# Negated maxima sent earlier, loads and stores given behind them, weight conversions in two halves: a block-sparse attention and feed-forward kernel

## The chip, the cores and the metric

The kernel runs as one launch on one core of one Trainium2 chip. The metric is the time of the launch on the device in microseconds (us); the median of several runs counts. The engines are named as in the profile: PE (matrix products), PEld (its weight loads), DVE (vector), ACT (scalar), POOL (GpSimd) and SP (which here only issues DMA transfers). On-chip memory is SBUF; products of PE land in PSUM, eight banks of 128 x 512 words.

## What is computed

Attention over 4 batches of 8 heads, 768 positions, 64 numbers per position, with a mask by blocks of 32 positions; its output is the input of a feed-forward part.

```python
scores = scale * np.matmul(q, k.transpose(0, 1, 3, 2))
...
mask = np.abs(blk_i - blk_j) <= window
mask = mask | (blk_i == 0) | (blk_j == 0) | (blk_i == n_blocks - 1) | (blk_j == n_blocks - 1)
...
scores = np.where(mask, scores, -1000000000.0)
scores = scores - np.max(scores, axis=-1, keepdims=True)
attn = np.exp(scores)
attn = attn / (np.sum(attn, axis=-1, keepdims=True) + 1e-09)
return np.matmul(attn, v).astype(np.float32)
...
h = x @ w_in
g = h - np.tanh(h)
return (g @ w_out).astype(np.float32)
```

The feed-forward part takes the 3072 positions as rows of 512 numbers, and its weights are 512 x 2048 and 2048 x 512. The weights arrive as 64-bit words and are turned into 32-bit ones by integer operations on DVE.

## The kernel before

The 32 heads are worked in 16 **pairs**. A head has three **double tiles** n (96 in all): two tiles of 128 rows against 768 columns, which take three PSUM banks of 512 columns. So a pair has six double tiles. For each double tile n:

- `smax` makes the masked scores once, roughly (one product of 88 rows per piece), into a bank, and `most` takes the maximum of each row from it on DVE (tile mc). This runs about six double tiles (one pair) ahead of use: the constant LEAD is 12, and a double tile lasts two units of the order's time.
- `scores` makes them again, finely: two products per piece, of which the second reads 89 rows of a **slot**. Row 88 of the slot holds the negated maximum, so the product delivers scores less their maximum. `exps` takes the exponential on ACT (tile pe), `high` (ACT, ph) and `low` (POOL, pl) split it into two halves of 16 bits, and `accum` multiplies these with v on PE.

Behind the three double tiles of a head in `smax`, the maxima go into row 88: `most_join` (DVE, tile mj), `most_turn` (PE, a transposition into a PSUM bank) and `most_send`: DVE negates and scales (tile nm), and SP sends the 3 KB into the slot. The second product of the next `scores` that needs this head waits for that transfer.

Ahead of that, a pair's inputs are prepared: `load_x` fetches q and k (tile rawx, 768 KB), `mask_words` and `low_words` split them on DVE in three parts each (the upper words into a PSUM bank, the lower into tile lo), `dist` sends them into the pair's slot in twelve transfers of 192 KB (letters A to D from rawx, c and d from lo). `load_v` fetches v (tile rawv, 384 KB); `v_most`, `v_turn`, `v_scale` and `v_parts` scale it by its maximum (tile am) and split it into the tile vhl. `norm` divides the output of a head by its sum (tile xq), and `spill` stores the output of a pair (384 KB) to `xscr` in memory.

Beside the attention, six pieces of weights are loaded (`load_pre`, 512 KB each, in tile rawi or rawo, one every 24 units) and converted by `convert_pre`, in three operations of DVE over 512 columns (`convert_op`), with a PSUM bank in between. The result (tile cvti or cvto) is stored to memory (`wt`) and read when the attention ends.

**What sets the order.** All engine instructions of the attention are written out by a list of due times: `at(time, f, *args)` puts a step into the list, the list is sorted, and the class `InOrder` (its line 79 issues everything, which is why the profile shows L79) keeps each engine to this program order. A pair has 12 units. The times decide the order alone; when a step runs is decided by waits. Six PSUM banks are given out in turn (`bank()`) to `scores`, `smax`, `mask_words`, `most_turn`, `v_turn` and the conversions, so a step that is moved also changes who waits for whose bank. SP issues its transfers in that order, and one behind another.

The first pairs have shifts of their own (LATE), and `smt(n)` spreads the first 24 double tiles. Behind the attention (from about 415 us) the feed-forward part runs, whose code the change doesn't touch.

## Time and profile before

| | us |
|---|---|
| median of 3 runs | 967.9 (965.65 to 968.12) |
| profiled execution | 962.25 |
| its span | 960.2 |
| PE busy | 891.2 |
| DVE busy | 736.6 |
| ACT busy | 642.7 |
| POOL busy | 474.8 |

The profile is of one execution. In the row of DMA below, the span is cut into 40 slices of 24 us, and each digit is the share in tenths that the 16 DMA engines were busy: they are nearly full during the attention (the first 17 slices) and mostly idle afterwards.

```
PE   2798899899989989779999999999999999999997
DVE  6798999899999977279999766766666675666664
ACT  0587889899989989855666665555555565555453
DMA  8946778877877783343622120310010010001001
```

### The profile page before, as it was taken

The numbers are of one execution on the slowest core, as the hardware profiler recorded it, in microseconds if no ns is written. First come the engines' busy times: TensorE is split into PE (matmuls) and PEld (weight loads), VectorE is DVE, ScalarE is ACT, GpSimd is POOL, SyncE is SP. The second block draws the span as 40 slices with busy tenths as digits, with TensorE's granted clock in tenths as the row PEclk, the third lists the DMA queues.
The fourth block names the chain that finished last, engine by engine and source line by source line (L and its number), as shares of the span: only waits on it lengthen the run. The fifth ranks groups of instructions, "written<-read, shape, count | busy, mean of one in ns | idle before, by whom it ended". The sixth has DMA issues, their size and how long they took to land.

```text
span 960.2 us, 18142 instructions
## 1 busy us (share of the span) xinstructions
PE 891.2 (93%) x7072; PEld 740.1 (77%) x7072; DVE 736.6 (77%) x1254; ACT 642.7 (67%) x1045; POOL 474.8 (49%) x231
## 2 busy tenths in 40 slices
PE   2798899899989989779999999999999999999997
PEld 1676778787878778667888788888888888888885
DVE  6798999899999977279999766766666675666664
ACT  0587889899989989855666665555555565555453
POOL 1376889788989888934455322222222222222221
PEclk9998999999999999889999999999999999999999
DMA  8946778877877783343622120310010010001001
GB/s 212 215 106 172 190 200 206 195 198 201 200 192 192 194 177 115 107 141 118 193 94 75 39 63 1 110 34 1 20 58 0 1 44 1 1 0 45 1 1 44
DMA packets 54101, 99.75 MB, mean 104 GB/s; under 512 B 5768, under 2 KB 26440, under 8 KB 54016
## 3 DMA queue, kind: packets, MB, share of 16 engines
q1 hardware_dynamic: 53704, 97.81, 38.3%
q8 instruction: 55, 0.90, 0.4%
q10 hardware_dynamic: 312, 0.79, 0.3%
q14 instruction: 30, 0.25, 0.1%
HBM read 44.64 MB, written 15.20 MB: 62 GB/s over the span
## 4 chain that ended last, share of the span: by engine, by line
PE 73%; DVE 11%; DMA 7%; ACT 4%; issue 3%; POOL 1%; SPq 0%; DVEq 0%; ACTq 0%; POOLq 0%
PE pf L563 25%; PE ps L79 24%; PE pf L595 8%; PE pf L596 8%; PE pf L597 8%; DMA slot<-nm 3%; DVE mc L79 3%; ACT pe L79 2%; DVE ps L79 2%; DMA slot<-lo 1%; PE pf L477 1%; DVE vhl L79 1%; POOL pl L79 1%; DMA slot<-rawx 1%; DVE pf L579 1%
## 5 line engine op out<-in xcount | busy, mean ns | idle before, releaser
L79 POOL TENSOR_TENSOR pl<-pe,ph 128x1536 f16<-128x1536 f32 x96 | 308.0, 3214 | 90.6 <-ACT ph L79 67.2
L79 PE MATMUL ps<-slot 89*128 89x512 f32 (+5 forms) x1152 | 254.0, 365 | 43.4 <-DMA slot<-nm 14.3
L586 POOL TENSOR_TENSOR gl<-t,gh 128x512 fp32r<-128x512 f32 x94 | 121.4, 1292 | 346.0 <-ACT gh L585 290.3
L79 PEld LDWEIGHTS ps<-slot 89*128 89x128 f32 (+2 forms) x1152 | 182.3, 199 | 72.1 <-DMA slot<-nm 18.2
L79 DVE TENSOR_REDUCE mc<-ps 128x1 f32<-128x512 f32 (+1 forms) x288 | 188.4, 682 | 31.1 <-PE ps L79 29.0
L79 ACT ACTIVATE pe<-ps 128x512 f32<-128x512 f32 x288 | 166.1, 588 | 42.0 <-PE ps L79 37.8
L79 ACT ACTIVATE ph<-pe 128x768 f16<-128x768 f32 x192 | 161.8, 843 | 5.6
L578 DVE TENSOR_TENSOR t<-t,pf 128x512 f32<-128x512 f32 x94 | 64.4, 685 | 124.6 <-ACT t L572 124.6
L585 ACT ACTIVATE gh<-t 128x512 fp32r<-128x512 f32 x94 | 59.4, 632 | 118.8 <-DVE t L582 118.7
L79 PEld LDWEIGHTS <-ph 128*128 128x128 f16 x2304 | 112.9, 99 | 25.8 <-issue 25.3
L79 PE MATMUL ps<-vhl,ph 128*128 128x65 f16 (+1 forms) x2304 | 124.7, 197 | 2.5 <-DVE vhl L79 1.9
L79 PE MATMUL ps<-vhl,pl 128*128 128x65 f16 x1152 | 119.6, 195 | 5.5 <-POOL pl L79 5.5
L79 PEld LDWEIGHTS <-pl 128*128 128x128 f16 x1152 | 109.0, 101 | 7.9 <-POOL pl L79 7.9
L570 ACT ACTIVATE u<-pf 128x512 f32<-128x512 f32 x94 | 56.2, 598 | 77.1 <-PE pf L563 76.4
L595 PE MATMUL pf<-wx,gh 128*128 128x512 f32 x192 | 74.7, 389 | 0.0
L596 PE MATMUL pf<-wx,gh 128*128 128x512 f32 x192 | 74.7, 389 | 0.0
L582 DVE COPY_PREDICATED t<-mk,pf 128x512 f32<-128x512 int32 x94 | 69.5, 740 | 6.6
L581 DVE SCALAR_TENSOR_TENSOR pf<-qq,pf 128x512 f32<-128x512 f32 x94 | 65.2, 693 | 7.8 <-DVE pf L580 0.5
L563 PE MATMUL pf<-slot,wx 128*128 128x512 f32 x288 | 70.3, 391 | 0.4 <-DVE t L582 0.4
L563 PE MATMUL pf<-xbuf,wx 128*128 128x512 f32 x288 | 69.5, 390 | 0.0
L574 ACT ACTIVATE qq<-u,bias 128x512 f32<-128x512 f32 x94 | 68.3, 727 | 0.0
L576 ACT ACTIVATE mk<-u,bias 128x512 f32<-128x512 f32 x94 | 67.8, 721 | 0.0
(113 smaller groups left out, 1468.5 us busy)
## 6 DMA issues: line engine op xcount, KB each, us to landing
slot<-rawx SPq DMA_DIRECT2D x128, 192.0 KB
slot<-lo SPq DMA_DIRECT2D x64, 192.0 KB
rawx<-kq SPq DMA_DIRECT2D x15, 768.0 KB
stage<-w_in SPq DMA_DIRECT2D x13, 512.0 KB
stage<-w_out SPq DMA_DIRECT2D x13, 512.0 KB
rawv<-v SPq DMA_DIRECT2D x16, 384.0 KB
xscr<-xq SPq DMA_DIRECT2D x16, 384.0 KB
out<-ob SPq DMA_DIRECT2D x24, 256.0 KB
```

The lines of the kernel that those rows point to most:

```text
L79: r = f(*args, **kw)
L563: nc.tensor.matmul(h, lhsT=w[:, cc], rhs=x[:, c, :], start=(k == 0), stop=(k == 3 * NCT - 1))
L574: nc.scalar.activation(out=qq, in_=u, func=AF.Square, scale=QS, bias=qbias)
L576: nc.scalar.activation(out=mk, in_=u, func=AF.Relu, scale=-1.0, bias=tbias)
L578: nc.vector.tensor_tensor(out=t, in0=t, in1=h, op=ALU.subtract)
L581: nc.vector.scalar_tensor_tensor(out=h, in0=qq, scalar=QC, in1=h, op0=ALU.add, op1=ALU.mult)
L582: nc.vector.copy_predicated(t, mk.bitcast(I32), h)
L585: nc.scalar.activation(out=gh, in_=t, func=AF.Copy)
L586: nc.gpsimd.tensor_tensor(out=gl, in0=t, in1=gh.bitcast(F32), op=ALU.subtract)
L595: nc.tensor.matmul(o, lhsT=gh[:, c], rhs=wo[0][ft], start=(ft == f0), stop=False)
L596: nc.tensor.matmul(o, lhsT=gh[:, c], rhs=wo[1][ft], start=False, stop=False)
L597: nc.tensor.matmul(o, lhsT=gl[:, c], rhs=wo[0][ft], start=False, stop=(ft == f1 - 1))
```

## The change

Four numbers in the list of due times, and a split. The load of x stands 1.8 units later (-34.2 for -36), the store of xq 3.2 units later (19.6 for 16.4). From the fifth head on, the turn of the maxima and their sending stand 1.2 units sooner (`late` 0.8 for 2). And each weight conversion is done in two halves of 256 columns, the second four units behind the first, each with three operations and a bank of its own; the store stands behind the second half.

```diff
-        at(t0 - 36 + late[0] if pr > 1 else -18.5 if pr else -49, load_x, pr)
+        at(t0 - 34.2 + late[0] if pr > 1 else -18.5 if pr else -49, load_x, pr)
...
-        at(t0 + 16.4, spill, pr)
+        at(t0 + 19.6, spill, pr)
...
-        late = 0 if h < 4 else 2
+        late = 0 if h < 4 else 0.8
         at(t0 + 1.6, most_join, h)
         at(t0 + 2.5 + late, most_turn, h)
         at(t0 + 2.75 + late, most_send, h)
...
-    def convert_pre(m, ft, k):
+    def convert_pre(m, ft, e, k):
         if k == 0:
-            wcv[m, ft] = f2.tile([P, 512], I32, tag="wcvt", name=f"cvt{m}{ft}")
-            wcp[0] = bank().bitcast(I32)
-        convert_op(nc, wraw[m, ft], wcv[m, ft], wcp[0], k)
-        if k == 2:
+            if e == 0:
+                wcv[m, ft] = f2.tile([P, 512], I32, tag="wcvt", name=f"cvt{m}{ft}")
+            wcp[0] = bank()[:, 0:256].bitcast(I32)
+        convert_op(nc, wraw[m, ft][:, 512 * e : 512 * (e + 1)], wcv[m, ft][:, 256 * e : 256 * (e + 1)], wcp[0], k)
+        if e and k == 2:
             nc.sync.dma_start(out=wt[m, ft], in_=wcv.pop((m, ft)).bitcast(F32))
...
-        for k in range(3):
-            at(W0 + DW * x + 6.05 + 0.45 * k, convert_pre, "io"[x % 2], x // 2, k)
+        for e in range(2):
+            for k in range(3):
+                at(W0 + DW * x + 6.05 + 4 * e + 0.45 * k, convert_pre, "io"[x % 2], x // 2, e, k)
```

**SP's queue in pair 9**, from nm of an odd head (nm19) on to the load of x behind; `slot2_75<-rawx11` and `slot2_75<-lo11` are the transfers of pair 11's q and k, `rawo1<-w_out` is a weight load, `xscr2<-xq8` the store of pair 8, `rawv11` the load of v. Before:

```order
L79 DMA slot0_73<-nm19_4021 1x6x128
L79 DMA slot2_75<-rawx11_3518 64x768 x2
L79 DMA xscr2_62<-xq8_3873 768x1x128
L79 DMA slot2_75<-rawx11_3518 64x768 x2
L79 DMA rawo1_4167<-w_out 128x1024
L79 DMA slot2_75<-rawx11_3518 64x768 x2
L79 DMA rawv11_4226<-v 128x768
L79 DMA slot1_74<-nm20_4232 1x6x128
L79 DMA slot2_75<-rawx11_3518 64x768 x2
L79 DMA slot2_75<-lo11_3745 64x768 x2
L79 DMA rawx13_4357<-kq 128x1536
```

After:

```order
L79 DMA slot0_73<-nm19_4010 1x6x128
L79 DMA rawx12_4016<-kq 128x1536
L79 DMA slot1_74<-lo10_3327 64x768
L79 DMA slot2_75<-rawx11_3595 64x768 x4
L79 DMA rawo1_4175<-w_out 128x1024
L79 DMA slot2_75<-rawx11_3595 64x768
L79 DMA slot1_74<-nm20_4222 1x6x128
L79 DMA xscr2_62<-xq8_3882 768x1x128
L79 DMA slot2_75<-rawx11_3595 64x768
L79 DMA rawv11_4239<-v 128x768
L79 DMA slot2_75<-rawx11_3595 64x768 x2
```

Both nm stand further ahead: the store, one of the slot transfers and the load of v now stand behind nm20, and the load of x (rawx12) stands behind nm19, where it stood ahead of it.

**SP's queue early**, about nm2 (head 2), which is not moved. Before:

```order
L79 DMA rawx3_420<-kq 128x1536
L79 DMA rawv2_434<-v 128x768
L79 DMA slot2_75<-rawx2_241 64x768
L79 DMA slot1_74<-nm2_489 1x6x128
L79 DMA slot2_75<-rawx2_241 64x768 x5
```

After:

```order
L79 DMA rawv2_432<-v 128x768
L79 DMA slot2_75<-rawx2_277 64x768
L79 DMA slot1_74<-nm2_487 1x6x128
L79 DMA rawx3_495<-kq 128x1536
L79 DMA slot2_75<-rawx2_277 64x768 x5
```

The load of x for pair 3 went from ahead of nm2 to behind it.

**DVE at a conversion**, in pair 6 (rawo0 is the weight piece, mc14 the maxima of head 14, nm13 the negated maxima of head 13, am7 the maximum of v). Before:

```order
L79 TENSOR_SCALAR ps3_97<-rawx8_2260 128x512
L79 TENSOR_TENSOR lo8_2483<-rawx8_2260,ps3_97 128x512
L79 TENSOR_SCALAR ps5_99<-rawo0_2489 128x512
L79 TENSOR_REDUCE mc14_2690<-ps2_96 128x2
L79 SCALAR_TENSOR_TENSOR ps5_99<-rawo0_2489,ps5_99 128x512
L79 TENSOR_REDUCE mc14_2690<-ps0_94 128x1
L79 SCALAR_TENSOR_TENSOR cvto0_2699<-rawo0_2489,ps5_99 128x512
L79 TENSOR_REDUCE mc14_2690<-ps2_96 128x1
L79 TENSOR_REDUCE am7_2762<-rawv7_2548 128x1
L79 TENSOR_SCALAR nm13_2766<-ps4_98 6x128
```

After:

```order
L79 TENSOR_SCALAR ps4_98<-rawx8_2332 128x512
L79 TENSOR_TENSOR lo8_2485<-rawx8_2332,ps4_98 128x512
L79 TENSOR_SCALAR ps0_94<-rawo0_2491 128x256
L79 TENSOR_REDUCE mc14_2691<-ps3_97 128x2
L79 SCALAR_TENSOR_TENSOR ps0_94<-rawo0_2491,ps0_94 128x256
L79 TENSOR_REDUCE mc14_2691<-ps1_95 128x1
L79 TENSOR_SCALAR nm13_2747<-ps2_96 6x128
L79 SCALAR_TENSOR_TENSOR cvto0_2700<-rawo0_2491,ps0_94 128x256
L79 TENSOR_REDUCE mc14_2691<-ps4_98 128x1
L79 TENSOR_REDUCE am7_2767<-rawv7_2555 128x1
```

Each conversion operation here has half the columns, nm13 stands four places further ahead, in front of am7, and the other three operations follow two double tiles later.

## The prediction

> **What bounds the kernel now.** I read the stretches by pair first, then what PE waits for, then the queue of SP at one of those waits. The stage behind 415 us is not touched by the change, so everything is looked for ahead of it. The stretches are cut where ScalarE starts the first exponential of a pair of heads; the columns are the stretch, its length, busy time of PE, PEld, DVE, ACT and POOL (with instructions), PE's clock, DMA share and GB/s.

> ```profile
> core 0: us, PE busy (x) PEld busy (x) DVE busy (x) ACT busy (x) POOL busy (x), PEclk, DMA share, GB/s
> 109.65:132.46 22.81, 20.91 (x294) 17.63 (x293) 20.34 (x40) 20.30 (x32) 20.22 (x7) 1.00 0.81 196
> ...
> 155.09:178.09 23.00, 20.89 (x294) 17.53 (x293) 20.46 (x41) 20.48 (x32) 21.48 (x8) 1.00 0.87 204
> ...
> 200.70:221.76 21.06, 20.65 (x294) 17.69 (x293) 19.98 (x40) 20.40 (x32) 19.30 (x7) 1.00 0.83 201
> 221.76:244.36 22.60, 21.22 (x294) 17.61 (x293) 21.69 (x43) 20.59 (x33) 19.31 (x7) 1.00 0.76 203
> 244.36:266.97 22.61, 20.93 (x294) 17.63 (x293) 20.20 (x41) 20.50 (x32) 20.77 (x8) 1.00 0.82 190
> ...
> 333.17:357.79 24.62, 20.78 (x294) 17.56 (x293) 18.98 (x37) 20.27 (x32) 22.71 (x8) 1.00 0.73 156
> ```

> These are pairs 3, 5, 7, 8, 9 and 13. Pair 7 is a plain one: 21.06 us, with PE, ACT and DVE all within 1.1 us of full. Pair 8 holds a weight conversion: 1.54 longer, with DVE 1.71 busier. Pairs 3, 5, 9 and 13 are 1.75, 1.94, 1.55 and 3.56 longer than pair 7, though PE, DVE and ACT do hardly more. What PE waits for between 120 and 360 us (total, times, longest), and the steps of the chain at two of these places:

> ```profile
> PE ps L79 <- DMA slot<-nm: 6.8, 3, 3.8
> PE ps L79 <- ACT pe L79: 3.6, 9, 0.4
> PE ps L79 <- DMA slot<-rawx: 1.9, 1, 1.9
> PE ps L79 <- DVE cvti L79: 1.4, 2, 0.7
> PE ps L79 <- DVE cvto L79: 1.4, 2, 0.7
> ...
> 259.06 7.27 DMA slot<-nm
> 347.81 9.34 DMA slot<-nm
> ```

> The negated maxima (nm, 3 KB) take over 7 us to arrive, and the second half of the scores needs them. The 1.9 us in pair 3, put down to a transfer of rawx, stand before the same matmul; by the code the rawx transfers sent then fill the slot of a later pair, so I count it with the nm waits. SP's queue around 259 shows why they are late:

> ```profile
> 249.57 0.74 SPq L79 DMA_DIRECT2D slot<-nm  x1
> 250.35 1.13 SPq L79 DMA_DIRECT2D slot<-rawx  x2
> 251.65 0.57 SPq L79 DMA_DIRECT2D xscr<-xq  x1
> 252.27 2.18 SPq L79 DMA_DIRECT2D slot<-rawx  x2
> 254.49 0.59 SPq L79 DMA_DIRECT2D rawo<-w_out  x1
> 255.18 1.39 SPq L79 DMA_DIRECT2D slot<-rawx  x2
> 256.67 0.54 SPq L79 DMA_DIRECT2D rawv<-v  x1
> 259.06 0.74 SPq L79 DMA_DIRECT2D slot<-nm  x1
> ```

> and the same places in stretches of 2 us (columns as above):

> ```profile
> 248.00:250.00 2.00, 2.00 (x38) 1.67 (x37) 2.00 (x4) 1.96 (x4) 2.00 (x1) 1.00 0.23 50
> ...
> 258.00:260.00 2.00, 1.60 (x11) 1.20 (x9) 1.83 (x5) 1.97 (x5) 1.07 (x1) 1.00 1.00 264
> ```

> Nm of the odd head (249.57) leaves into a queue that is drained (DMA share 0.23); nm of the even head (259.06) leaves behind six transfers of 192 KB, a store and v of 384 KB each and a weight load of 512 KB, 2432 KB, with the share at 1.00.

> **The change, part by part.** The span is 960.2 and its execution 962.25, 5.65 under the median of 967.9; the sum is made against 962.25, and the 5.65 are added at the end.

> *Nm sooner, load and stores behind it.* On PE and DVE nm is moved, nothing is added:

> ```profile
> 249.27 0.27 DVE L79 TENSOR_SCALAR nm<-ps 6x128 fp32r<-6x128 f32 x1
> ...
> 255.41 0.68 DVE L79 TENSOR_SCALAR ps<-rawx 128x512 int32<-128x512 int32 x1
> ...
> 258.76 0.27 DVE L79 TENSOR_SCALAR nm<-ps 6x128 fp32r<-6x128 f32 x1
> ```

> The odd nm goes from behind am, the maximum of v, to behind the third mc of the tile before: from 249.27 to about 247.7, 1.6 us. The even one comes in front of the masks of the next tile, about 0.8 us. Between the two nm the queue now holds the load of x (768 KB), six transfers (1152 KB) and the weights (512 KB): again 2432 KB, but they start 1.6 us sooner, at about 248.7. If the even nm lands 1.6 sooner, the waits of pairs 5 and 9 (excess 1.94 and 1.55) and of pair 3 (1.75) shrink to 0.3 at most. In pair 13 no load of x is left, and store and v, 768 KB, are now behind nm: at the 264 GB/s above that is 3 us, with the 0.8 us enough for its 3.56. The excess of the four is 8.80. Bounds: all of it, or pair 13's alone (3.56), if the early start is eaten by the load of x. I take **-8.0**.

> *Banks.* Six PSUM banks go round in program order, so moving the turn of nm changes which score waits for which reader:

> ```profile
> 215.63 0.98 PE L79 MATMUL ps<-slot 128*128 128x512 f32 x3 [0.41 <-ACT pe L79]
> ```

> Before, the turn and a mask word take two banks between the first and third score of a tile, so the third gets the first one's bank and waits 0.41 us for its exponential. With the turn in the tile before, it gets nm's, which has been read by then. Nine such waits are listed (3.6 us). ACT is 20.40 of 21.06 busy in a plain pair, so part comes back as a later wait: between 0 and -3.6, taken **-2.0**, in the middle.

> *Conversions in halves.* Three operations over 512 columns become six over 256. Duration of the whole, and the rows of similar operations with fewer columns:

> ```profile
> L79 DVE SCALAR_TENSOR_TENSOR ps<-rawi,ps 128x512 int32<-128x512 int32 x3 | 2.1, 686 | 0.0
> ...
> L79 DVE TENSOR_TENSOR xq<-ps,rs 128x384 f32<-128x384 f32 x23 | 12.8, 558 | 0.8
> ...
> L79 DVE TENSOR_REDUCE sb<-ps 128x1 f32<-128x128 f32 x11 | 3.1, 280 | 0.0
> ```

> A half lies between 0.280 and 0.558; I take 0.42, the middle. Six are 2.52, three were 2.06: DVE gets 0.46 more per conversion, but in two tiles. The burst, in which two score banks wait 0.7 us each (the four waits on cvti and cvto above), is cut. Six conversions lie in pairs 4 to 14, each at 1.54 over a plain pair. Bounds: a gain of 1 us each (-6, two thirds of the excess), or the added DVE time with no gain (+2.8). Since DVE's total rises and it is 21.69 of 22.60 busy, I stay near a third of a us each: **-2.0**. [...]

> *The load of x for pair 3* is the one place where the moved load meets its reader:

> ```profile
> 38.23 0.72 SPq L79 DMA_DIRECT2D rawx<-kq  x1
> ...
> 50.31 0.78 SPq L79 DMA_DIRECT2D slot<-nm  x1
> ...
> 53.79 0.69 DVE L79 TENSOR_SCALAR ps<-rawx 128x512 int32<-128x512 int32 x1
> ...
> 419.12 3.05 DMA xscr<-xq
> 422.36 3.83 DMA stage<-w_in
> ```

> Before it leaves at 38.23. After, it stands behind nm of head 2, so at about 51.1. 384 KB took 3.05 and 512 KB 3.83 in a free queue; the same slope gives an estimate of 5.4 for 768 KB, so it lands at 56.5 and the mask word of 53.79 waits 2.7 us. DVE is the engine that PE waits for there. Bounds: +1.5 (nm, moved by nothing here, but DVE late anyway) and +2.7; taken **+2.4**.

> In the steady pairs the same load leaves 6.3 us later than before (about 248.75, from 242.44) for a mask word at 255.41: it has 6.66 us and needs 5.4, so it is costed at nothing, with 1.2 us of cover. The store of xq and the store of converted weights move away from the even nm; both are read again at the end of the attention stage or behind it (the last weights stored at 173 units of the order's time, read at 181), so they cost nothing.

> Sum: -8.0 - 2.0 - 2.0 + 2.4 = **-9.6**; 962.25 - 9.6 = 952.65, and with 5.65 a median of **958.3**.

> **Rivals.**

> *(a) The load of x comes late in every pair (slower).* It decides if the load takes more than 6.66 us from nm: DVE then stands at the mask word, and behind it all mc and the next nm. For it: the even nm took 7.27 us in a full queue. Against: the odd nm leaves in a drained one, and a tail that delays nm shows that what is issued first is served first. If it lands like that nm or somewhat later, at 8.5 us, DVE loses 1.8 us in each of 11 pairs, +20: about 978. 6%.

> *(b) DVE's second part of v misses POOL (slower).* Rows of DVE and POOL:

> ```profile
> 73.87 3.41 DVE L79 SCALAR_TENSOR_TENSOR vhl<-rawv,sb,vhl 128x768 f16<-128x768 f32 x1
> ...
> 217.75 1.43 DVE L79 SCALAR_TENSOR_TENSOR vhl<-rawv,sb,vhl 128x768 f16<-128x768 f32 x1
> ...
> 215.23 6.92 POOL L79 TENSOR_TENSOR pl<-pe,ph 128x1536 f16<-128x1536 f32 x2 [1.08 <-PE ps L79]
> ```

> The same operation took 3.41 us early and 1.43 in a steady pair, where it starts within the first of POOL's two operations (3.46 each) and ends 0.5 after its end. Should it come 0.9 us later against POOL, it would meet the second one whole, up to 3.4 us instead of 1.43: 2 us in some 9 pairs, +18, about 976. Against: nm no longer stands ahead of it, which makes it earlier. 6%. [...]

> *(c) Nm still waits behind the same bytes.* The queue between the two nm is 2432 KB before and after; if the load of x runs slower than what it replaces, only the gains of banks and conversions are left, against the loss at pair 3: -2.0 - 2.0 + 2.4 = -1.6, 966.3. Against: in pair 13 the bytes do go. 12%.

> *(d) DVE is full.* The halves cost 0.46 us each, +2.8 for six, and no bank wait is gained: -8.0 + 2.8 + 2.4 = -2.8, 965.1. 6%.

> **How the numbers follow.** The forecast has 70%, the rivals 6, 6, 12 and 6. What a measurement tells from no change is 0.3%, 2.9 us, so faster means under 965.0. The forecast is under it nearly whole (68 of 70), with a fifth of (c) and half of (d): 0.73. Within 2.9 us: the rest of (c), of (d) and of the forecast, 0.15. Slower: (a) and (b), 0.12. The range holds the forecast with its terms half way to their good ends (-8.8, -2.8, -4, +2: -13.6, 954.3, and 1.8 for the spread of the runs) and reaches to (c): 952.5 to 966.5.

> **What would show it.** Right: PE's waits on nm between 120 and 360 under 1 us; pairs 5, 9 and 13 within 0.5 us of pair 7; no PE wait of 0.41 on ACT; conversion pairs under 22.3; one DVE idle of some 2.5 us before a mask word near 54. Wrong: DVE idle before mask words in steady pairs (a), v's second part over 2 us (b), nm landing after 264.5 in the place of 266.3 (c), DVE over 21.9 busy in conversion pairs of unchanged length (d).

## The result and the profile after

| | before | after |
|---|---|---|
| median, us | 966.77 (4 runs, 964.02 to 968.12) | 953.68 (4 runs, 952.32 to 955.48) |
| ratio to before | | 0.9887, 95% interval 0.9847 to 0.9928 |
| profiled execution, us | 962.25 | 955.48 |
| its span, us | 960.2 | 953.5 |

The change takes 13.1 us off the medians. The forecast was 958.3 in a range of 952.5 to 966.5. The two profiled executions differ by only 6.8 us: that of before lies below its median, that of after is the slowest of its four. A second profile of the changed kernel (below, `a0_after`) has a span of 951.6.

Of the 6.7 us between the two spans, pairs 3 to 13 give 10.5 (from 109.65 to 357.79 before, from 116.69 to 354.35 after), the start takes 7.0 back, and 3.2 lie behind pair 13, most of them in the feed-forward part, whose code is the same. Behind the last exponential of the attention the twelve profiles of this case take 552.6 to 556.5 us, and the two profiles of the changed kernel alone differ there by 1.7, so that the 3.1 of them between these two need not be the change's. The 10.5 is what the second profile repeats (10.3).

The stretches by pair of the changed kernel, cut and with columns as those shown of before (pairs 3, 4, 5, 7, 8, 9 and 13):

```profile
116.69:137.46 20.77, 20.77 (x297) 17.91 (x296) 19.74 (x39) 20.16 (x31) 18.24 (x6) 1.00 0.77 191
137.46:161.42 23.96, 22.27 (x292) 18.57 (x291) 22.01 (x45) 20.14 (x33) 18.97 (x7) 0.93 0.73 184
161.42:182.69 21.27, 21.27 (x295) 17.89 (x294) 20.30 (x41) 20.25 (x32) 19.59 (x7) 1.00 0.83 218
204.69:225.60 20.91, 20.91 (x294) 17.72 (x293) 19.97 (x40) 20.12 (x32) 19.25 (x7) 1.00 0.86 217
225.60:247.57 21.97, 21.37 (x294) 17.81 (x293) 21.59 (x46) 20.25 (x32) 19.26 (x7) 1.00 0.73 195
247.57:268.55 20.98, 20.98 (x294) 17.69 (x293) 19.96 (x40) 20.14 (x33) 19.25 (x7) 1.00 0.83 213
333.41:354.35 20.94, 20.94 (x296) 17.79 (x295) 18.82 (x36) 20.07 (x32) 19.24 (x7) 1.00 0.81 206
```

Pairs 3, 5, 9 and 13 (22.81, 23.00, 22.61 and 24.62 before) have no idle PE left: 20.77, 21.27, 20.98 and 20.94, 9.08 us less in all. The conversion in pair 8 fell from 22.60 to 21.97. Two things are worse: pair 3 begins at 116.69 and no longer at 109.65, and pair 4 takes 23.96, with a clock of 0.93. Pair 4 before:

```profile
132.46:155.09 22.63, 22.22 (x294) 19.00 (x293) 21.52 (x41) 20.53 (x32) 17.38 (x6) 0.92 0.70 190
```

Its clock was no better before, behind the wait of 1.9 us in pair 3. That wait is gone, but PE is idle for 1.69 us in pair 4 now, where it was for 0.41. What PE waits for between 126 and 360 us in the changed kernel:

```profile
PE ps L79 <- DVE mc L79: 2.1, 4, 0.5
PE ps L79 <- DVE cvti L79: 1.7, 1, 1.7
```

The rows on nm, on rawx and on ACT are gone. SP's queue in pair 9, from one nm to the next:

```profile
251.53 0.74 SPq L79 DMA_DIRECT2D slot<-nm  x1
252.39 0.36 SPq L79 DMA_DIRECT2D rawx<-kq  x1
...
256.56 1.09 SPq L79 DMA_DIRECT2D rawo<-w_out  x1
257.75 0.90 SPq L79 DMA_DIRECT2D slot<-rawx  x1
261.66 0.74 SPq L79 DMA_DIRECT2D slot<-nm  x1
262.45 0.57 SPq L79 DMA_DIRECT2D xscr<-xq  x1
```

The last transfer ahead of the even nm is given 3.9 us before it, and store and v come behind it. The loss at the beginning, in rows of DVE and PE of the changed kernel:

```profile
58.63 0.69 DVE L79 TENSOR_SCALAR ps<-rawx 128x512 int32<-128x512 int32 x1 [2.90 <-DMA rawx<-kq]
```
```profile
60.70 3.78 PE L79 MATMUL ps<-slot 128*128 128x512 f32 x11 [4.57 <-DVE mc L79]
```
```profile
58.00:60.00 2.00, 0.00 (x0) 0.00 (x0) 1.34 (x3) 0.00 (x0) 2.00 (x1) 0.73 1.05 228
60.00:62.00 2.00, 1.30 (x3) 1.11 (x4) 1.84 (x4) 0.00 (x0) 0.57 (x1) 0.50 0.46 97
62.00:64.00 2.00, 2.00 (x9) 1.81 (x9) 1.58 (x3) 1.33 (x3) 0.00 (x0) 0.50 0.02 6
64.00:66.00 2.00, 2.00 (x30) 1.48 (x29) 2.00 (x4) 1.97 (x3) 0.00 (x0) 0.56 0.00 0
```

DVE stands 2.90 us for pair 3's load of x, PE stands 4.57, and PE's granted clock is 0.50 from 58.92 to 65.75, for 6.83 us, in 5.05 of which PE works. So this stall of PE costs more than its own 4.57 us. That is the second cost that the experiments follow.

### The profile page after: what moved, and what is told of

Its sections match the earlier page's. It is cut to its first block, busy times and chain, and to the rows that moved or that the text cites. A ratio compares the mean times of both kernels' runs of the same rounds, so it can differ in the third digit from the quotient of the medians.

```text
span 953.5 us, 18150 instructions
## 1 busy us (share of the span) xinstructions
PE 892.2 (94%) x7072; PEld 740.4 (78%) x7072; DVE 734.5 (77%) x1272; ACT 639.1 (67%) x1045; POOL 474.2 (50%) x231
## 4 chain that ended last, share of the span: by engine, by line
PE 78%; DVE 10%; DMA 7%; ACT 3%; issue 1%; SPq 1%; POOL 0%; DVEq 0%
PE ps L79 26%; PE pf L565 26%; PE pf L597 8%; PE pf L598 8%; PE pf L599 8%; DVE mc L79 3%; DMA slot<-lo 2%; DMA slot<-nm 1%; DVE ps L79 1%; ACT pe L79 1%; SPq L79 1%; DVE vhl L79 1%; PE pf L479 1%; DMA rawv<-v 1%; DMA slot<-wo 1%
## 5 line engine op out<-in xcount | busy, mean ns | idle before, releaser
L79 POOL TENSOR_TENSOR pl<-pe,ph 128x1536 f16<-128x1536 f32 x96 | 307.2, 3210 | 86.6 <-ACT ph L79 69.4
L79 PE MATMUL ps<-slot 89*128 89x512 f32 (+5 forms) x1152 | 254.4, 366 | 36.0 <-DVE mc L79 14.2
L79 PEld LDWEIGHTS ps<-slot 89*128 89x128 f32 (+2 forms) x1152 | 181.6, 200 | 68.6 <-DVE mc L79 23.5
L79 DVE TENSOR_REDUCE mc<-ps 128x1 f32<-128x512 f32 (+1 forms) x288 | 188.4, 681 | 20.6 <-PE ps L79 19.9
L79 ACT ACTIVATE pe<-ps 128x512 f32<-128x512 f32 x288 | 163.9, 587 | 40.5 <-PE ps L79 37.8
L79 ACT ACTIVATE ph<-pe 128x768 f16<-128x768 f32 x192 | 161.8, 843 | 5.6
L79 PEld LDWEIGHTS <-ph 128*128 128x128 f16 x2304 | 114.8, 99 | 20.6 <-issue 17.0
L79 PE MATMUL ps<-vhl,ph 128*128 128x65 f16 (+1 forms) x2304 | 124.4, 197 | 2.1 <-DVE vhl L79 1.5
L79 PE MATMUL ps<-vhl,pl 128*128 128x65 f16 x1152 | 119.8, 195 | 5.1 <-POOL pl L79 5.1
L79 PEld LDWEIGHTS <-pl 128*128 128x128 f16 x1152 | 109.0, 101 | 7.1 <-POOL pl L79 7.1
```

The source lines that it names most:

```text
L79: r = f(*args, **kw)
```

## The experiments

Ten experiments ran in three groups (two of them run a kernel once more); a group shares its runs of before. Differences are of medians in a group, or of ratios to before between groups.

| kernel | median, us | before | ratio, 95% interval |
|---|---|---|---|
| `e1_x3_back` | 949.1 | 964.14 | 0.985 (0.9822 to 0.9878) |
| `e2_nm_alone` | 959.21 | 964.14 | 0.995 (0.992 to 0.9979) |
| `e3_loads_alone` | 957.71 | 964.14 | 0.9948 (0.992 to 0.9976) |
| `e4_halves_alone` | 959.78 | 964.14 | 0.9945 (0.9925 to 0.9965) |
| `a0_after` | 952.92 | 963.53 | 0.9888 (0.9856 to 0.9921) |
| `e5_no_halves` | 963.6 | 963.53 | 0.9991 (0.9965 to 1.0017) |
| `e6_x_back` | 951.22 | 963.53 | 0.9855 (0.9821 to 0.9888) |
| `e7_x_back_conv` | 949.22 | 963.53 | 0.9846 (0.9812 to 0.988) |
| `e8_x3_conv` | 947.67 | 965.16 | 0.9824 (0.9799 to 0.985) |
| `e10_no_halves_again` | 963.39 (one run) | 965.16 | |

### What one late load costs: `e1_x3_back`

```diff
-        at(t0 - 34.2 + late[0] if pr > 1 else -18.5 if pr else -49, load_x, pr)
+        at(t0 - (36 if pr == 3 else 34.2) + late[0] if pr > 1 else -18.5 if pr else -49, load_x, pr)
```

> The change as it is, but the load of x for pair 3 alone goes back to its old place, ahead of nm of head 2. Theory (that one load costs its wait, and the wait costs clock besides): in the changed kernel DVE idles 2.90 us at 55.73 for that load, PE idles 4.57 at 56.13, and then the granted clock is 0.50 from 59 to 65; all this goes, PE's idle near 55 falls to some 1.6 as before the change, and the time falls by 5 to 7 from 953.7, to 947 to 949. Rival 1 (only the wait itself is lost): 2.4 to 2.9 less, about 951. Rival 2 (the early loss comes from elsewhere, from nm of head 1 at 42.67 or the lo tile at 83): the time stays within 1 us of 953.7, since another stall takes the place.

Measured: ratio 0.985 against 0.9887 and 0.9888 of the changed kernel in the other two groups, 3.6 us of 964; pair 3 begins at 108.10, against 116.69 and 112.07 in the two profiles of the changed kernel. PE's row at the place that had 4.57 us, before the change and in this kernel:

```profile
55.85 2.45 PE L79 MATMUL ps<-slot 128*128 128x512 f32 x11 [1.59 <-DVE mc L79]
```
```profile
54.32 1.97 PE L79 MATMUL ps<-slot 128*128 128x512 f32 x9 [1.59 <-DVE mc L79]
```
```profile
54.00:56.00 2.00, 1.68 (x9) 1.54 (x10) 2.00 (x5) 0.70 (x2) 1.91 (x1) 0.88 0.35 78
56.00:58.00 2.00, 2.00 (x16) 1.38 (x15) 1.97 (x5) 1.94 (x4) 1.21 (x1) 0.50 0.00 0
58.00:60.00 2.00, 2.00 (x33) 1.87 (x31) 1.58 (x3) 0.74 (x2) 1.13 (x1) 0.76 0.00 0
```

The stall is 1.59, as before the change, and the slow clock behind it lasts 3.41 us, as before the change, where the changed kernel had 6.83. The theory holds in kind; 3.6 us by the ratios is less than the 5 to 7 expected, and the intervals overlap, so its size is not settled: the wait alone is 2.9 us, and at the start of pair 3 this profile is 4.0 ahead of the second profile of the changed kernel. The 8.6 to the first profile are more than this load costs: ahead of the load's wait, from 38.44 to 48.68, the first profile has a clock of 0.50 and this one 1.00. One row of this kernel also shows the rival (a) of the prediction, once, in pair 5:

```profile
166.66 0.69 DVE L79 TENSOR_SCALAR ps<-rawx 128x512 int32<-128x512 int32 x1 [2.15 <-DMA rawx<-kq]
```

### The parts alone: `e2_nm_alone`, `e3_loads_alone`, `e4_halves_alone`

Nm alone is, in the kernel before:

```diff
-        late = 0 if h < 4 else 2
+        late = 0 if h < 4 else 0.8
```

> The kernel before with nm alone 1.2 units sooner (load, store and conversions as before). Theory (nm is late because of what SP gave out ahead of it): ahead of the even nm now stand 2048 KB and no longer 2432, and it leaves 0.8 us sooner, so the waits on nm in pairs 5, 9 and 13 fall from 6.8 us in all to under 1.5, the bank waits of 0.41 go, and nothing is lost early: 966.8 less 9 to 11, 956 to 958. Rival (the load and the store behind nm do it): waits on nm stay above 4 us in all, the time is 962 to 965.

The waits are as the theory has them: between 120 and 360 us PE has no row on nm and none on ACT. The time is not: 4.9 us less, not 9 to 11. The gain is given back in the conversion pairs. Stretches of pairs 8 and 10, and PE in pair 8:

```profile
222.09:246.40 24.31, 22.93 (x294) 19.15 (x293) 21.93 (x43) 20.37 (x32) 19.25 (x7) 0.93 0.65 179
267.39:290.17 22.78, 21.38 (x294) 17.88 (x293) 21.76 (x43) 20.36 (x33) 19.24 (x7) 1.00 0.67 184
```
```profile
225.89 1.46 PE L79 MATMUL ps<-slot 128*128 128x512 f32 x7 [0.81 <-DVE mc L79]
227.87 1.76 PE L79 MATMUL ps<-slot 88*128 88x256 f32 x5 [0.51 <-DVE cvti L79]
```
```profile
228.00:230.00 2.00, 2.00 (x15) 1.38 (x16) 2.00 (x4) 1.58 (x3) 0.98 (x1) 0.57 0.65 193
```

With nm sooner, a whole conversion stalls PE by 0.81 and 0.51 us, 2 us apart, and in pair 8 the granted clock is then 0.50 for 3.4 of the 4 us from 228 to 232 (means of 0.57 and 0.58): 24.31 us. Pair 10 has the same two stalls and no slow clock: 22.78.

Load and store alone are, in the kernel before:

```diff
-        at(t0 - 36 + late[0] if pr > 1 else -18.5 if pr else -49, load_x, pr)
+        at(t0 - 34.2 + late[0] if pr > 1 else -18.5 if pr else -49, load_x, pr)
...
-        at(t0 + 16.4, spill, pr)
+        at(t0 + 19.6, spill, pr)
```

> The kernel before with load of x and store moved alone (nm and conversions as before). Theory (what matters is what stands ahead of nm): the load of x, 768 KB, now stands right ahead of the odd nm, and the even nm has its 2432 KB as before; the odd nm lands 5 us or more after it is sent instead of 1.8, and its scores come 4.5 us behind its sending, so waits appear at odd heads too; with the loss at pair 3 the time goes up by 5 to 20, to 972 to 987. Rival (the moved load and store empty the queue for nm by themselves): nm waits shrink, time 958 to 966.

This expectation was wrong. The kernel is 6.4 us faster than before, although pair 3 begins at 116.71. Between 120 and 360 us PE waits 1.5 us for nm, not 6.8, and SP's queue in pair 9 shows the error:

```profile
PE ps L79 <- DMA slot<-nm: 1.5, 2, 1.0
```
```profile
246.66 0.38 SPq L79 DMA_DIRECT2D rawx<-kq  x1
247.09 0.47 SPq L79 DMA_DIRECT2D slot<-lo  x1
253.72 0.74 SPq L79 DMA_DIRECT2D slot<-nm  x1
...
257.88 0.88 SPq L79 DMA_DIRECT2D slot<-rawx  x1
258.85 0.57 SPq L79 DMA_DIRECT2D xscr<-xq  x1
```

The load of x is next to the odd nm in the order but 7 us ahead of it in time, since SP stands at nm until DVE has made it; by then the DMA engines are idle (share 0.00 from 252 to 254). And the store, 384 KB, is no longer ahead of the even nm. In pair 13, without a load of x, the wait of 3.84 us went wholly (20.72 us). So either part, nm or loads, takes most of the nm waits by itself; together they don't gain twice.

The halves alone are the changed kernel with the three numbers of load, store and nm put back.

> The kernel before with the conversions in halves alone. Theory (the burst on DVE makes a conversion pair longer, and halves cut it): pairs 6, 8, 10 and 12 fall from 22.6 to about 22.0 each, as in the changed kernel, and the time by 2 to 4, to 963 to 965. Rival 1 (DVE is full and the halves give the gain back): no change, 966 to 969. Rival 2 (the shorter conversion pairs of the changed kernel come from nm's and the bank's new place): pairs stay at 22.4 to 22.8.

Measured 4.4 us less. Pairs 6, 8 and 12 fall to 21.87, 21.85 and 21.87, by 0.73 to 0.75, with nm in its old place; pair 10 does not (22.64), as its clock is slow for 3.41 us behind a wait on nm in pair 9. Pairs 6 and 8:

```profile
176.97:198.84 21.87, 21.32 (x294) 17.59 (x293) 21.37 (x45) 20.49 (x31) 19.03 (x7) 1.00 0.74 203
219.98:241.83 21.85, 21.29 (x294) 17.59 (x293) 21.47 (x46) 20.49 (x32) 19.19 (x7) 1.00 0.77 200
```

Both rivals fall: the halves work by themselves.

### The moves without the halves: `a0_after`, `e5_no_halves`, `e10_no_halves_again`

> The changed kernel once more, beside the others of this group and with a second profile. Theory (the early loss belongs to the kernel, not to one execution): pair 3 begins at 114 to 118 us as in the first profile (116.69; before 109.65), pairs 6 to 13 take 20.9 and 22.0 in turn; ratio to before 0.984 to 0.992. Rival (the early loss was one execution's): pair 3 begins near 110 and the time is some 5 lower, as the other timed runs would then be.

The ratio came out at 0.9888. Pair 3 begins at 112.07, 2.4 us behind the 109.65 of before and not 7.0: the stall is there again (PE idle 4.80 at 54.03), and so are the 6.83 us of slow clock behind it. The first profile has 10.2 us more at the slow clock elsewhere ahead of pair 3 (10.24 for 3.41 at 38 to 49, 6.83 for 3.41 at 86). So the early loss belongs to the kernel, and a part of its size to the execution.

`e5_no_halves` is the kernel before with both edits shown above (nm, and load and store).

> Nm sooner and load and store moved, but conversions whole. Theory (with nm sooner the whole burst stalls PE and can slow its clock, as with nm alone, where conversion pairs took 22.7 or, with a granted clock of 0.50 behind the stall, 24.3): pairs 6, 8, 10 and 12 at 22.7 to 24.4 instead of 21.97, the time 3 to 9 above the changed kernel. Rival (the halves don't matter once nm and the loads are moved): pairs at 22.0, the time within 1.5 of the changed kernel.

963.6 against 963.53 before: without the halves the moves gain nothing that can be measured, and the halves are worth 10.7 us on top of them (952.92). In its profile pairs 6, 8, 10 and 12 took 22.75 to 22.80; that execution took 961.42 at a mean clock of 0.985, and others of the ten took up to 966.6, at 0.975 to 0.978. A second profile of the same kernel:

> The kernel with nm, load and store moved and whole conversions, looked at once more. Theory (in a conversion pair PE idles 0.81 and 0.52 us close together, and in some executions the clock answers with 0.50 for about 3 us): in at least one of pairs 6, 8, 10 and 12 the pair takes 24.2 to 24.4 with a granted clock of 0.50 behind the second idle time, the others 22.75; the mean clock is under 0.982. Rival (what the timed runs lost against the first profile lies in the early pairs or in the last stage): all four at 22.75, the difference before pair 3 or behind pair 15.

Stretches of pairs 6, 8, 10 and 12, PE in pair 6, and the stretches of 3.41 us about the two stalls in pair 6 and in pair 8:

```profile
179.75:203.98 24.23, 22.91 (x295) 19.18 (x294) 21.80 (x43) 20.46 (x32) 19.19 (x7) 0.93 0.69 178
224.91:247.68 22.77, 21.37 (x294) 17.89 (x294) 21.66 (x43) 20.39 (x33) 19.24 (x7) 1.00 0.72 188
268.65:292.94 24.29, 22.92 (x294) 19.12 (x293) 21.95 (x43) 20.36 (x33) 19.25 (x7) 0.93 0.68 171
314.39:337.09 22.70, 21.38 (x295) 17.95 (x294) 21.69 (x43) 20.47 (x33) 19.19 (x7) 1.00 0.76 201
```
```profile
183.50 1.46 PE L79 MATMUL ps<-slot 128*128 128x512 f32 x7 [0.80 <-DVE mc L79]
185.47 0.98 PE L79 MATMUL ps<-slot 88*128 88x256 f32 x3 [0.52 <-DVE cvto L79]
```
```profile
182.37:185.78 3.41, 2.09 (x20) 1.62 (x17) 3.41 (x7) 2.16 (x4) 3.41 (x2) 1.00 0.12 33
185.78:189.20 3.42, 3.42 (x42) 2.80 (x40) 2.29 (x4) 2.12 (x3) 1.51 (x2) 0.50 0.66 155
226.74:230.15 3.41, 2.60 (x44) 2.15 (x42) 3.38 (x8) 2.06 (x4) 3.41 (x2) 1.00 0.30 76
230.15:233.57 3.42, 2.90 (x45) 2.48 (x45) 3.39 (x7) 2.88 (x4) 1.92 (x2) 1.00 0.39 60
```

Two of four conversion pairs take 24.2 and 24.3, at the slow clock, the others 22.7, as expected. This is most of the missing gain: nm stands in the middle of the whole conversion's burst now, PE stalls twice in a short time there, and the clock takes 1.5 us more in some of these pairs. Against the second profile of the changed kernel, pairs 4, 6, 8, 10 and 12 take 6.9 us more here, 0.8 each by the longer stalls and 1.5 in two of them by the clock; in the first profile of the kernel without halves they take 4.0 more, and none of 6 to 12 is slow. In pair 5 another 2.1 us here are DVE's wait of 2.24 for a late load of x, which the first profile has not. What is left of the 10.7 us is not attributed. The start costs both kernels alike: pair 3 begins at 113.55 and 110.78 without the halves. With halves and nm sooner the pairs have one stall of 0.54, and none of the pairs 6 to 12 shows a slow clock in those six profiles (in the first of the changed kernel it is 1.00 from 147.67 to 393.43).

### Must the load of x stand behind nm: `e6_x_back`

The changed kernel with -36 again for all loads of x.

> The changed kernel with the load of x back at its old place in all pairs (nm sooner, store moved and halves kept). Theory (nm sooner, with store and v behind it, is enough; the load of x ahead of the odd nm does no harm, since the odd nm has about 6 us, and the move of the load costs the early stall): no PE wait on nm from 120 to 360, the odd nm lands within 3.3 us, the early stall goes; 5 to 8 below the changed kernel of this group, like the kernel with pair 3's load alone put back or 1 to 2 better. Rival (the load of x had to go behind nm): waits on nm of 0.5 us or more in most pairs, the time above that of pair 3's load alone put back by 3 or more.

1.7 us below the changed kernel, not 5 to 8. The early stall went (pair 3 begins at 110.16), but in the pairs that load w_in, 7 and 11, PE now waits for the odd nm. SP and PE in pair 7:

```profile
201.02 0.34 SPq L79 DMA_DIRECT2D rawx<-kq  x1
201.41 0.47 SPq L79 DMA_DIRECT2D slot<-lo  x1
202.14 0.75 SPq L79 DMA_DIRECT2D slot<-nm  x1
```
```profile
208.74 0.50 PE L79 MATMUL ps<-slot 89*128 89x512 f32 x1 [0.46 <-DMA slot<-nm]
```

Here the load stands right ahead of nm in time too, and nm arrives 6.6 us later, just too late. So with nm sooner the move of the load is worth 0.7 to 0.8 us in each of these two pairs of this profile, and hurts at pair 3. In the next kernel, whose loads stand as here, pair 7 has no such wait and pair 11 one of 0.23.

### The first conversion, and both repairs: `e7_x_back_conv`, `e8_x3_conv`

`e7_x_back_conv` is `e6_x_back` with:

```diff
-                at(W0 + DW * x + 6.05 + 4 * e + 0.45 * k, convert_pre, "io"[x % 2], x // 2, e, k)
+                at(W0 + DW * x + 6.05 + (0 if x else 0.5) + 4 * e + 0.45 * k, convert_pre, "io"[x % 2], x // 2, e, k)
```

> As the kernel with the load of x back in all pairs, and the first of the six conversions 0.5 units later, so that no mask word stands between its three operations. Theory (in pair 4 the bank of the half is held over a mask word and its low word, PE idles 1.7 us for it and its clock then is 0.50 for some 3 us): pair 4 falls from 23.9 to about 22.0, no slow clock there, time 1.5 to 2.5 lower. Rival 1 (only the wait itself is won): 1 us or less. Rival 2 (another bank takes its place): no change.

Pair 4 in `e6_x_back`, with PE's wait in it, and in `e7_x_back_conv`:

```profile
130.94:154.93 23.99, 22.28 (x292) 18.48 (x291) 22.04 (x45) 20.16 (x33) 19.00 (x7) 0.93 0.72 183
```
```profile
135.92 1.46 PE L79 MATMUL ps<-slot 128*128 128x256 f32 x8 [1.71 <-DVE cvti L79]
```
```profile
130.78:152.76 21.98, 20.86 (x292) 17.33 (x291) 21.53 (x46) 20.35 (x33) 19.34 (x7) 1.00 0.75 197
```

2.01 us less in the pair and 2.0 in the medians; the clock in the pair goes from 0.93 to 1.00. PE's whole idle time there fell by only 0.6 us (1.71 to 1.12, the stretch less PE's busy time): most of the gain is clock, not wait.

`e8_x3_conv` is the changed kernel with this edit and that of `e1_x3_back`.

> The changed kernel with two repairs: the load of x for pair 3 alone at its old place, and the first conversion 0.5 units later. Theory (the two losses are apart and add up): pair 3 begins near 109, pair 4 takes about 22.0, no nm wait in the pairs with a w_in load; ratio to before 0.980 to 0.984, 945 to 948. Rival (the early part is bound elsewhere, so that the repairs overlap or the later load is late now and then by 2 us at a mask word): 0.985 or more, no better than either repair alone.

Ratio 0.9824, the lowest of all, 947.67 against 965.16: better than the change as it was made, though its interval overlaps those of `e1_x3_back` and `e7_x_back_conv`. Pair 3 begins at 109.00, pair 4 takes 22.35, pairs 7 and 11 20.94 and 20.92. In pair 5 DVE stands 1.79 us before a mask word here too (its row names ACT as what ended the wait), and 2.15 in the first repair's profile, while the two profiles of the changed kernel have no such wait.

## Why the prediction was right, step by step

The time lies in the range and the sign is right; 4.6 us of the gain were not in the forecast (953.68 for 958.3).

- **Nm sooner, load and stores behind it** (-8.0). Right: 9.08 us in pairs 3, 5, 9 and 13, and no wait on nm is left. It went further than the working: the even nm was to land 1.6 us sooner behind the same 2432 KB, but the last of these bytes are given out 3.9 us ahead of it, before 2.4, and by the packets of the trace nm of pair 9 is through within 2 us of its issue, before after 5.9. The split between nm and the moves was not seen: either alone does most of it (`e2_nm_alone`, `e3_loads_alone`).
- **Banks** (-2.0). The waits of 0.41 went, all nine, but pair 7 gained only 0.15 (21.06 to 20.91). The term was mis-sized, near its lower end: PE has no idle time left in 20.91 us, where it had 20.65 busy before.
- **Conversions in halves** (-2.0). By themselves -4.4. In the changed kernel pairs 6, 8, 10 and 12 gained 0.6 each, and pair 4 lost 1.33 (22.63 to 23.96) by a new wait of 1.7 us for the bank of a half, which no term had (`e7_x_back_conv`). The duration of a half was right: 420 ns for the first two operations. What failed is that the step counted the halves on their own: moving nm would have made the whole conversion stall PE twice and, in some pairs, slow its clock, so that the halves are what lets the other moves pay (10.7 us).

```profile
L79 DVE TENSOR_SCALAR ps<-rawi 128x256 int32<-128x256 int32 x6 | 2.5, 420 | 0.0
```

- **The load of x for pair 3** (+2.4). The wait was 2.90 us, forecast 2.7; the loss in the time is larger, 3.6 us by the ratios, because PE's stall was 4.57, before 1.59, and the slow clock behind it 6.83, before 3.41. That the term came near is in part luck: the prediction priced a stall by its length alone and left the clock out.
- **The offset** of 5.65 between profile and median. The profiles alone give -6.8, or -8.7 with the second one (953.52); the medians give -13.1 and -10.6 in two groups. The forecast's -9.6 lies between them, which is in part luck: 3 us of the first profile's gain lie in the feed-forward part, and the start lost 2.4 us in one profile and 7.0 in the other. How far an execution's clock falls is a difference that the runs show (means of 0.975 to 0.985 in the ten runs of `e5_no_halves`); why the changed kernel's median is nearer to its profiles than that of before was not settled.
- **Rivals.** (a), a late load of x, did come, but once, for 2.15 us in pair 5 of `e1_x3_back` and 2.24 in that of `e10_no_halves_again`, whose other profile has none; not in every pair. (b) did not: v's second part takes 1.30 to 1.52 us in the steady pairs; the 3.4 that it was to take there was the author's estimate from one early row (3.41 us at 73.87), and none of these pairs shows it. (c) did not: no wait on nm is left. (d) did not: DVE is 21.59 of 21.97 busy in pair 8, fuller than before, and the pair is shorter.

## What to carry to other kernels

A place in a queue's order is not a time: ask when the queue's engine comes to the instruction, and what it stands at until then, before pricing what is "ahead" of it. Where a trace shows an engine's clock fall behind a stall (here to 0.50 for 3.41 us behind 1.59 us of standing, `e1_x3_back`), price the stall with the slow stretch behind it, and take two short stalls close together as one (here 0.80 and 0.52 us, with the same 3.41 us behind them, pair 6 of `e10_no_halves_again`). A part of a change that gains little alone can be what makes another part pay, so try the parts without it, not only by themselves.

## What the hardware showed

From its first record on (33.62 us before, 31.62 after) PE's granted clock is 1.00 or 0.50 in these two profiles. It changed only at borders that lie whole multiples of 3.41 us apart (before at 40.45, 43.86, 57.52, 60.93, 78.00, 84.82, 132.61, 136.02 and so on, after at 38.44, 48.68, 58.92, 65.75, 86.23, 93.06, 144.26, 147.67 and so on), and its stretches at 0.50 are 3.41, 6.83 or 10.24 us long (the last of each profile is cut by its end). It fell 2.8 to 3.7 us after the beginning of an idle time of 4.57 us (`after`, at 56.13), 1.59 (`e1_x3_back`, at 52.74), 1.71 (`e6_x_back`, pair 4), 4.80 (`a0_after`, at 54.03), and of 0.80 and 0.52 with 1.5 us of work between (`e10_no_halves_again`, pair 6).
